# Moving batch 1's norm check and batch 0's first block scaling to VectorE, with new load times and pairs of score units, in a fused attention and FFN kernel

## The chip, the cores and the metric

The kernel runs on one core of one Trainium2 chip. The metric is device time in microseconds (us): the median of several executions. Engine names: PE is TensorE's matrix multiplication (PEld its weight loads, which overlap it), DVE is VectorE, ACT is ScalarE, POOL is GpSimd, SP is SyncE, which here only issues DMA transfers.

## The reference, cut to what matters

Eight batches of causal attention with a decay bias (8 heads, 576 positions, 64 columns per head) feed an RMS norm and a gated FFN over 4608 tokens.

```python
scores = scale * q @ k.T                                  # per batch and head
scores = where(causal, -1e9, scores + minimum(-(cum_i - cum_j), 0))
attn   = softmax(scores)                                  # [8, 8, 576, 576]
x      = (attn @ v) -> [4608, 512]
xn     = x / sqrt(mean(x*x) + 1e-6) * rms_g
out    = (silu(xn @ w_gate) * (xn @ w_val)) @ w_out       # d_ff = 1536
```

Of the kernel before, what the change touches and what calls it, by code (L numbers as in the profile page):

```python
# [270 lines left out]
def kernel(  # L271
# [13 lines left out]
    fp32 = mybir.dt.float32  # L285
    bf16 = mybir.dt.bfloat16
    i32 = mybir.dt.int32
    AF = mybir.ActivationFunctionType
    ALU = mybir.AluOpType
    AX = mybir.AxisListType  # L290

    B, H, S, D = q.shape
    DM = 512
    DF = 1536
# [3 lines left out]
    KC = 9  # L298
# [12 lines left out]
    NRUN = 2  # L311
    LEAD = 0.5
    MARGIN = 3.0
    NTWO = 2
    NPE = 3

    pers = ctx.enter_context(tc.tile_pool(name="pers", bufs=1))
# [17 lines left out]
    half = pers.tile([BH, 1], fp32, name="half")  # L335
    wT = pers.tile([128, NB, BH], bf16, name="wT")
    nrm = pers.tile([128, 2, B, 3], fp32, name="nrm")
    rnrm = pers.tile([128, NRUN, 5], fp32, name="rnrm")
    rtop = pers.tile([128, 1], fp32, name="rtop")
    top = pers.tile([128, 2], fp32, name="top")  # L340
    mhalf = pers.tile([128, 3], fp32, name="mhalf")
# [40 lines left out]
    def I(eng, method, us, key=None, kind=None, dma=0.0, lags=(1.2, 1.2), **kw):  # L382
        outs = [kw[n] for n in ("out", "accum_out") if n in kw]
        ins = [a for n, a in kw.items()
               if n not in ("out", "accum_out") and isinstance(a, (bass.AP, View))]
        f = getattr(ENG[eng], method)
        o = R.add(eng, us, lambda: f(**{n: real(a) for n, a in kw.items()}), outs, ins, key=key,  # L387
                  lat=LAT[eng], kind=kind, dma=dma,
                  name=outs[0].bank.name if isinstance(outs[0], View) else outs[0].name)
        o.lags = lags  # L390
        return o

    def fill(eng, ap, value, us, key=None):
        f = ENG[eng].memset
        return R.add(eng, us, lambda: f(ap, value), [ap], [], key=key, lat=LAT[eng], name=ap.name)
# [34 lines left out]
    def load_runs(b, which, h0, h1, key, part=0):  # L430
        c0, c1 = PARTS[part] if b == 0 else (0, KC)
        p0 = KP * which
        us = ((1.2, 1.25)[part] * (h1 - h0) / 4) if b == 0 else 3.05 * (h1 - h0) / 8
        return I("pool", "dma_start", 0.7, key=key, dma=us, lags=(1.1, 1.2),
                 out=raw[b][part][p0 : p0 + KP, h0:h1, :, :].rearrange("p h c d -> p h (c d)"),
                 in_=(k, q)[which][b, h0:h1, KP * c0 : KP * c1, :].rearrange(
                     "h (p c) d -> p h (c d)", c=c1 - c0))
# [9 lines left out]

    def load_w(which, lo, hi, key):
        if which == 2:
            return I("pool", "dma_start", 0.84, key=key, dma=7.2 * (hi - lo) / 12,  # L450
                     out=wout_sb[:, lo:hi, :],
                     in_=moe_w_out[lo * 128 : hi * 128, :].rearrange("(fc p) d -> p fc d", p=128))
        dst, src = ((wg_sb, moe_w_gate), (wv_sb, moe_w_val))[which]
        return I("pool", "dma_start", 0.76, key=key, dma=8.1 * (hi - lo) / DF,
                 out=dst[:, :, lo:hi],
                 in_=src[:, lo:hi].rearrange("(cc p) f -> p cc f", p=128))

# [17 lines left out]
    def prep_cast(b, key):  # L475
        for sc in range(NB):
            n = 128 if sc < 4 else 64
            for src, dst, out in ((k_nat, k_bf, KT[b % 2]), (q_nat, q_bf, QT[b % 2])):
                I("dve", "tensor_copy", 0.34, key=key + sc, out=dst[0:n, sc], in_=src[0:n, sc])
                I("sp", "dma_start_transpose", 1.31, key=key + sc, dma=0.65,  # L480
                  lags=(0.5, 0.9 + 0.6 * MARGIN),
                  out=out[:, :, sc * 128 : sc * 128 + n], in_=dst[0:n, sc])
# [5 lines left out]
        I("act", "activation", 1.17 if w > DM else 0.74, key=key, out=sq_scr[0:n, 0:w], in_=src,  # L488
          func=AF.Square, accum_out=nrm[0:n, which, b, i : i + 1])

    def raw_norm(b, key):
        src = flat[b]
        for i in range(5):
            w = min(1024, H * KC * D - 1024 * i)
            I("act", "activation", 1.17 if w > DM else 0.74, key=key, out=sq_scr[:, 0:w],
              in_=src[:, 1024 * i : 1024 * i + w], func=AF.Square,
              accum_out=rnrm[:, b, i : i + 1])

    def prep_v(b, sc, eng, key):
        n = 128 if sc < 4 else 64  # L500
# [15 lines left out]
    def decay(key):  # L516
        I("dve", "tensor_scalar", 0.5, key=key, out=s_all, in0=s_all, scalar1=0.0, scalar2=None,
          op0=ALU.max)
        I("dve", "tensor_tensor_scan", 1.3, key=key, out=cum, data0=ones[:, 0:1].to_broadcast([BH, S]), data1=s_all, initial=0.0,
          op0=ALU.mult, op1=ALU.add)  # L520
        I("dve", "tensor_scalar", 0.1, key=key, out=half, in0=cum[:, S - 1 : S], scalar1=-0.5,
          scalar2=None, op0=ALU.mult)
        I("act", "activation", 0.7, key=key, kind="exp", out=w_row[:, 0:S], in_=cum, func=AF.Exp,
          bias=half, scale=1.0)
        tp = lay(bank("w", 1), fp32, "p (c b) -> p c b", n=NB * BH, c=NB)
        mms(0.6, [(tp[:, sc, :], w_row[:, sc * 128 : (sc + 1) * 128], ident_f, sc == 0,
                   sc == NB - 1, True) for sc in range(NB)], key=key)
        I("dve", "tensor_copy", 0.42, key=key, out=wT, in_=tp)
        return tp
# [125 lines left out]
    def att_out(b, tb, key):  # L655
        x = x_blk[b % 2][:, tb, :]
        if b >= NPE:
            p0 = 64 if tb == 4 else 0
            I("dve", "scalar_tensor_tensor", 0.66, key=key, out=x, in0=x,
              scalar=al[b % 2][:, 1, tb : tb + 1], in1=gB, op0=ALU.mult, op1=ALU.mult)  # L660
            c0 = b * S + tb * 128
            I("sp", "dma_start_transpose", 1.31, key=key - 3, dma=0.65, lags=(0.5, 0.9 + 0.6 * MARGIN),
              out=xnT[:, :, c0 : c0 + 128 - p0], in_=x_blk[b % 2][p0:128, tb, :])
            return
        if b == 0 and tb in (1, 3):
            I("dve", "tensor_scalar", 0.3, key=key, out=x, in0=x,
              scalar1=al[b % 2][:, 1, tb : tb + 1], scalar2=None, op0=ALU.mult)
        else:
            I("act", "activation", 0.72, key=key, out=x, in_=x, func=AF.Copy,
              scale=al[b % 2][:, 1, tb : tb + 1])  # L670
        p0 = 64 if tb == 4 else 0
        X = lay(bank("xt", 2) if b == 0 else small_bank(), bf16, "p (c t) -> p c t", n=DM, c=CC)
        mms(0.22, [(X[:, cc, :], x_blk[b % 2][:, tb, cc * 128 : (cc + 1) * 128], ident_bf,
                    cc == 0, cc == CC - 1, True) for cc in range(CC)], key=key)
        c0 = b * S + tb * 128
        I("dve", "tensor_tensor", 0.6, key=key, out=xnT[:, :, c0 : c0 + 128 - p0],
          in0=X[:, :, p0:128], in1=g_sb.unsqueeze(2).to_broadcast([128, CC, 128 - p0]),
          op=ALU.mult)
# [101 lines left out]
        fill("dve", t[64:128, 4, :, :], 0.0, 0.5, key=-90)  # L780
    fill("dve", mhalf, -0.5, 0.06, key=-90)
    fill("dve", nrm, 0.0, 0.08, key=-90)
    wP = decay(-95)
    for hp in range(HP):
        prep_transpose(0, hp, -80 + hp)
# [7 lines left out]
    norms = attention(0, -78, 3, 4)  # L793
    for o in vops[2:]:
        R.after(o, norms[3])
    raw_norm(0, 20)
    kq1 = [load_runs(1, w, h, h + 4, -45) for h in (0, 4) for w in range(2)]
    v1 = load_rows(v_nat[1 % len(v_nat)], v, 1, "pool", -44)
    w2 = [load_w(2, 6 * i, 6 * i + 6, -40) for i in range(2)]
# [4 lines left out]
    for c in range(NCH):  # L804
        K = PER * c
        plan = first if c == 0 else halves if c < 4 else whole
        for i, (o, n, f0) in enumerate(plan):
            ffn1_group(c, o, n, f0, K + STEP * 96 * i / len(plan))
        b = c + 1
        if b < B:  # L810
            if b < NRUN:
                for hp in range(HP):
                    prep_transpose(b, hp, K + hp)
            else:
                prep_cast(b, K - 14)
            if b < NRUN:
                raw_norm(b, K + 18)
            else:
                for i in range(3):
                    for w in range(2):  # L820
                        prep_norm(b, w, i, K + 20 + 2 * i)
            prep_w(b, "pool", K - 10)
            vops = [prep_v(b, sc, "pool", K - 8 + sc) for sc in range(NB)]
        if b + 1 < B:
            n = b + 1
            K2 = K - 14 + LEAD
            for sc in range(NB):
                for dst, src in ((k_nat, k), (q_nat, q)):
                    o = load_row(dst, src, n, sc, "sp", K2 + sc)
                    if n == NRUN:  # L830
                        R.after(o, *vops)
            lv = [load_row(v_nat[n % len(v_nat)], v, n, sc, "sp", K2 + 6 + sc) for sc in range(NB)]
            if n == NRUN:
                R.after(gl, *lv)
        if c == B - 1:
            check_decay(K + 10)
            check_all(K + 20)
        ffn2(c, K + STEP * 96, STEP)
        if b < B:
            attention(b, K + 1, 2.6, 2 if b > 3 else 4)  # L840
# [175 lines left out]
```

## The kernel before: the parts that the change touches

All work is written as operations with an estimated duration and a key. A planner written in Python replays them by these estimates, and from that it fixes the order on each engine and the places where PE gets dummy matmuls (`spin`) so that its clock stays up. The estimates therefore change no instruction, but they change the order of thousands.

```python
def load_runs(b, which, h0, h1, key, part=0):        # k and q of batches 0 and 1
    ...
    us = ((1.2, 1.25)[part] * (h1 - h0) / 4) if b == 0 else 3.05 * (h1 - h0) / 8
    return I("pool", "dma_start", 0.7, key=key, dma=us, lags=(1.1, 1.2), ...)

def raw_norm(b, key):                                # sums of squares for a range check
    src = flat[b]
    for i in range(5):
        w = min(1024, H * KC * D - 1024 * i)
        I("act", "activation", 1.17 if w > DM else 0.74, key=key, out=sq_scr[:, 0:w],
          in_=src[:, 1024 * i : 1024 * i + w], func=AF.Square,
          accum_out=rnrm[:, b, i : i + 1])

def att_out(b, tb, key):                             # scale a finished block of x by 1/rms
    x = x_blk[b % 2][:, tb, :]
    ...
    if b == 0 and tb in (1, 3):
        I("dve", "tensor_scalar", 0.3, key=key, out=x, in0=x,
          scalar1=al[b % 2][:, 1, tb : tb + 1], scalar2=None, op0=ALU.mult)
    else:
        I("act", "activation", 0.72, key=key, out=x, in_=x, func=AF.Copy, scale=...)
    # then: 4 PE transposes into PSUM, and one DVE product into xnT, the FFN's input

two = 2 if b >= NTWO else 1                          # NTWO = 2: score units in pairs from batch 2

def spin(b):                                         # a dummy matmul
    nc.tensor.matmul(b[:, 0:256], lhsT=still[:, 0:128], rhs=still, start=True, stop=True)
```

On POOL are the causal masks (`affine_select` on the exponentials `Ea` to `Eh`) and, from batch 1 on, the products of v with the decay weights (`vwb`).

## Time and profile before

| | before |
|---|---|
| median of 4 executions (358.43 to 359.1) | 358.69 us |
| span in the profiled execution | 356.3 us |
| PE busy | 342.1 us, 96% of the span |
| DVE / ACT / POOL busy | 70% / 65% / 38% |
| first attention-times-v matmul | 14.72 us |
| first FFN matmul | 23.50 us |

Since PE is at 96%, the time is PE's work, plus its idle time, plus whatever its work costs more at a lower clock. The lines that carry this stand in the prediction (in a timeline: start, duration, engine, line, operation, what it writes and reads). One more view of before is needed later, the timeline at 20 us (start, duration, engine, line, operation, what it writes and reads). It has the one scaling of a batch 0 block that DVE did already:

```profile
20.54 0.84 POOL L387 DMA_DIRECT2D wv_sb<-in_moe_w_val_dram  x1
20.61 0.45 DVE L387 TENSOR_SCALAR x_blka<-x_blka,ala 128x512 bf16<-128x512 bf16 x1
```

The scaling and a DMA issue of POOL run side by side, and the scaling takes 0.45 us. The same operation at 31.1 us took 0.35 us. I saw no meaning in this difference when I predicted.

### The profile page before, as it was taken

To read this page: it belongs to the slowest core of one execution; us is meant where nothing else is said; L and a number is where in the kernel's file an instruction comes from. 1 tells how busy PE (TensorE), PEld (TensorE's weight loads), DVE (VectorE), ACT (ScalarE), POOL (GpSimd) and SP (SyncE) were. 2 spreads that over 40 slices of the span, in tenths; PEclk is the share of its full clock that TensorE was granted. 3 is DMA by queue.
4 is the path that set the end of the run, shared out by engine and by line. 5 is a ranking of instruction groups with operands and counts; after the bars stand their busy time and mean duration, and the time that the engine had idled before them with its cause. 6 is when DMAs were issued, how large, how long until landed. Compare 5 with 4: busy or idle time off the path is not lost.

```text
span 356.3 us, 8029 instructions
## 1 busy us (share of the span) xinstructions
PE 342.1 (96%) x3016; PEld 209.5 (59%) x3016; DVE 250.4 (70%) x495; ACT 229.8 (65%) x472; POOL 134.9 (38%) x217
## 2 busy tenths in 40 slices
PE   5988999999999999999999999999999999999995
PEld 4667775698569874887544454455445444444443
DVE  4678856698748995879687868887588657806840
ACT  2688899595777995857685668666898433224321
POOL 8996377321381349013910293029325100000000
PEclk9799999999999999999999999999999999999999
DMA  7999999999899997998999996889730250020002
GB/s 116 182 183 209 224 200 213 182 215 187 177 185 213 179 193 135 211 175 156 153 215 156 182 159 159 193 166 133 195 62 2 32 156 2 0 89 31 0 31 94
DMA packets 140613, 51.14 MB, mean 144 GB/s; under 512 B 127380, under 2 KB 135320, under 8 KB 140568
## 3 DMA queue, kind: packets, MB, share of 16 engines
q1 hardware_dynamic: 131832, 41.13, 60.7%
q0 software_dynamic: 8736, 9.44, 16.0%
q8 instruction: 25, 0.41, 0.5%
q14 instruction: 20, 0.16, 0.2%
HBM read 38.16 MB, written 9.44 MB: 134 GB/s over the span
## 4 chain that ended last, share of the span: by engine, by line
PE 84%; DVE 6%; POOL 3%; issue 3%; ACT 2%; DMA 1%; SPq 0%; POOLq 0%; ACTq 0%; DVEq 0%
PE psa L404 11%; PE psd L404 11%; PE pse L404 11%; PE psh L404 10%; PE psg L404 10%; PE psb L404 10%; PE psc L404 9%; PE psf L404 8%; DMA q_nat<-in_q_dram 1%; DVE x_blka L387 1%; DVE x_blkb L387 1%; POOL q_nat L387 1%; ACT Ee L387 1%; DVE Hs L387 1%; PE psd L843 1%
## 5 line engine op out<-in xcount | busy, mean ns | idle before, releaser
L404 PEld LDWEIGHTS <-wg_sb 128*128 128x128 bf16 x624 | 60.0, 98 | 33.8 <-issue 2.1
L404 PEld LDWEIGHTS <-wv_sb 128*128 128x128 bf16 x624 | 59.8, 98 | 32.3 <-issue 1.5
L404 PEld LDWEIGHTS <-Hs 128*128 128x128 bf16 x444 | 41.4, 98 | 42.5
L387 POOL TENSOR_SCALAR_AFFINE_SELECT Eb<-Eb 128x512 bf16<-128x512 bf16 x8 | 5.4, 679 | 80.7 <-ACT Eb L387 80.7
L387 POOL TENSOR_TENSOR vwb<-v_nata,wT 128x512 bf16<-128x512 f32 (+1 forms) x20 | 20.4, 1047 | 0.0
L387 ACT ACTIVATE sq_scr<-x_blkb 128x512 bf16<-128x512 bf16 x20 | 12.7, 633 | 11.7 <-DVE x_blkb L387 11.3
L387 DVE SCALAR_TENSOR_TENSOR x_blkb<-x_blkb,alb,gB 128x512 bf16<-128x512 bf16 x15 | 12.2, 862 | 10.7 <-POOL alb L387 10.7
L404 PE MATMUL psd<-wout_sb,Hs 128*128 128x512 bf16 (+1 forms) x84 | 18.5, 364 | 0.0
L404 PE MATMUL psa<-wout_sb,Hs 128*128 128x512 bf16 x72 | 17.8, 379 | 0.0
L404 PE MATMUL pse<-xnT,wg_sb 128*128 128x256 bf16 (+1 forms) x100 | 17.6, 311 | 0.2 <-DVE u_sba L387 0.2
L404 PE MATMUL psh<-xnT,wv_sb 128*128 128x256 bf16 (+1 forms) x100 | 17.5, 311 | 0.2 <-DVE x_blkb L387 0.2
L404 PE MATMUL psa<-xnT,wv_sb 128*128 128x256 bf16 (+1 forms) x104 | 17.6, 306 | 0.0
L387 ACT ACTIVATE sq_scr<-x_blka 128x512 bf16<-128x512 bf16 x18 | 11.3, 630 | 9.3 <-DVE x_blka L387 8.9
L404 PE MATMUL pse<-wout_sb,Hs 128*128 128x512 bf16 x72 | 17.2, 379 | 0.0
L404 PE MATMUL psf<-xnT,wg_sb 128*128 128x256 bf16 (+1 forms) x88 | 16.5, 321 | 0.6 <-DVE xnT L387 0.6
L404 PE MATMUL psb<-xnT,wv_sb 128*128 128x256 bf16 (+1 forms) x88 | 16.5, 321 | 0.0
L387 ACT ACTIVATE sq_scr<-q_bf 128x1024 bf16<-128x1024 bf16 (+1 forms) x18 | 16.4, 909 | 0.1
L387 ACT ACTIVATE sq_scr<-k_bf 128x1024 bf16<-128x1024 bf16 (+1 forms) x18 | 16.3, 908 | 0.0
L387 DVE CAST q_bf<-q_nat 128x512 bf16<-128x512 f32 (+1 forms) x30 | 16.0, 532 | 0.6 <-DMA q_nat<-in_q_dram 0.6
L387 POOL TENSOR_TENSOR vwa<-v_nata,wT 128x512 bf16<-128x512 f32 (+1 forms) x15 | 15.8, 1078 | 0.9 <-DMA v_nata<-in_v_dram 0.7
L404 PE MATMUL psd<-xnT,wv_sb 128*128 128x256 bf16 (+1 forms) x88 | 14.5, 302 | 0.0
L404 PE MATMUL psb<-xnT,wg_sb 128*128 128x256 bf16 (+1 forms) x88 | 14.5, 302 | 0.0
(471 smaller groups left out, 879.4 us busy)
## 6 DMA issues: line engine op xcount, KB each, us to landing
v_nata<-in_v_dram SPq DMA_DIRECT2D x24, 256.0 KB, 5.1
k_nat<-in_k_dram SPq DMA_DIRECT2D x24, 256.0 KB, 3.7
q_nat<-in_q_dram SPq DMA_DIRECT2D x24, 256.0 KB, 4.3
out_dram<-osba SPq DMA_DIRECT2D x12, 256.0 KB, 2.3
out_dram<-osbb SPq DMA_DIRECT2D x12, 256.0 KB, 2.5
out_dram<-osbc SPq DMA_DIRECT2D x11, 256.0 KB, 2.3
v_nata<-in_v_dram POOLq DMA_DIRECT2D x8, 256.0 KB, 10.4
wout_sb<-in_moe_w_out_dram POOLq DMA_DIRECT2D x2, 768.0 KB, 16.6
```

The source lines that it names most:

```text
L387: o = R.add(eng, us, lambda: f(**{n: real(a) for n, a in kw.items()}), outs, ins, key=key, lat=LAT[eng], kind=kind, dma=dma, name=outs[0]. ...
L404: nc.tensor.matmul(out, lhsT=lhsT, rhs=rhs, start=st, stop=sp)
L843: nc.tensor.matmul(b[:, 0:256], lhsT=still[:, 0:128], rhs=still, start=True, stop=True)
```

## The change

Its intent is to take work off ACT, which was at 96% in two windows of batch 1, and to start the FFN earlier. It has five parts:

- (a) batch 1's norm check goes from ACT (5 pieces) to DVE (9 pieces of 512 columns)
- (b) batch 1's score units go in pairs
- (c) batch 0's first block of x is scaled on DVE
- (d) the planner gets new load times
- (e) batch 2's casts get a later key

What the change's name calls "v of batch 1 between the out weights' halves" is already in the load list of the kernel before; the diff does not touch it.

```diff
-    NTWO = 2
+    NTWO = 1
-    rnrm = pers.tile([128, NRUN, 5], fp32, name="rnrm")
+    rnrm = pers.tile([128, NRUN, 9], fp32, name="rnrm")
...  load_runs
-        us = ((1.2, 1.25)[part] * (h1 - h0) / 4) if b == 0 else 3.05 * (h1 - h0) / 8
+        us = ((1.05, 1.25)[part] * (h1 - h0) / 4) if b == 0 else 2.85 * (h1 - h0) / 8
...  load_w: 7.2 -> 7.5 for the out weights; lags=(1.2, 1.6) for the gate and value weights
...  prep_cast
-   I("dve", "tensor_copy", 0.34, key=key + sc, ...)
+   I("dve", "tensor_copy", 0.34, key=key + sc + (12 if b == NRUN else 0), ...)
...  raw_norm, new branch
+            else:
+                I("dve", "scalar_tensor_tensor", 0.66, key=key, out=x, in0=x, scalar=1.0, in1=x,
+                  op0=ALU.mult, op1=ALU.mult, accum_out=rnrm[:, b, i : i + 1])
...  att_out
-        if b == 0 and tb in (1, 3):
+        if b == 0 and tb in (0, 1, 3):
...  in the loop over batches (batch 1)
-                raw_norm(b, K + 18)
+                raw_norm(b, K + 23, "dve")
```

More of the change, by code (lines that the diff above doesn't have):

```diff
@@ L449, in load_w @@
         if which == 2:
-            return I("pool", "dma_start", 0.84, key=key, dma=7.2 * (hi - lo) / 12,
+            return I("pool", "dma_start", 0.84, key=key, dma=7.5 * (hi - lo) / 12,
                      out=wout_sb[:, lo:hi, :],
@@ L453, in load_w @@
         dst, src = ((wg_sb, moe_w_gate), (wv_sb, moe_w_val))[which]
-        return I("pool", "dma_start", 0.76, key=key, dma=8.1 * (hi - lo) / DF,
+        return I("pool", "dma_start", 0.76, key=key, dma=8.1 * (hi - lo) / DF, lags=(1.2, 1.6),
                  out=dst[:, :, lo:hi],
@@ L478, in prep_cast @@
             for src, dst, out in ((k_nat, k_bf, KT[b % 2]), (q_nat, q_bf, QT[b % 2])):
-                I("dve", "tensor_copy", 0.34, key=key + sc, out=dst[0:n, sc], in_=src[0:n, sc])
+                I("dve", "tensor_copy", 0.34, key=key + sc + (12 if b == NRUN else 0), out=dst[0:n, sc], in_=src[0:n, sc])
                 I("sp", "dma_start_transpose", 1.31, key=key + sc, dma=0.65,
@@ L489, in prep_norm, with raw_norm @@
           func=AF.Square, accum_out=nrm[0:n, which, b, i : i + 1])
-    def raw_norm(b, key):
-        src = flat[b]
-        for i in range(5):
-            w = min(1024, H * KC * D - 1024 * i)
-            I("act", "activation", 1.17 if w > DM else 0.74, key=key, out=sq_scr[:, 0:w],
-              in_=src[:, 1024 * i : 1024 * i + w], func=AF.Square,
-              accum_out=rnrm[:, b, i : i + 1])
+    def raw_norm(b, key, eng):
+        w = 1024 if eng == "act" else DM
+        for i in range(-(-H * KC * D // w)):
+            x = flat[b][:, w * i : min(w * i + w, H * KC * D)]
+            if eng == "act":
+                I("act", "activation", 1.17 if x.shape[1] > DM else 0.74, key=key,
+                  out=sq_scr[:, 0 : x.shape[1]], in_=x, func=AF.Square,
+                  accum_out=rnrm[:, b, i : i + 1])
+            else:
+                I("dve", "scalar_tensor_tensor", 0.66, key=key, out=x, in0=x, scalar=1.0, in1=x,
+                  op0=ALU.mult, op1=ALU.mult, accum_out=rnrm[:, b, i : i + 1])
     def prep_v(b, sc, eng, key):
@@ L782 @@
     fill("dve", nrm, 0.0, 0.08, key=-90)
+    fill("dve", rnrm, 0.0, 0.06, key=-90)
     wP = decay(-95)
@@ L795 @@
         R.after(o, norms[3])
-    raw_norm(0, 20)
+    raw_norm(0, 20, "act")
     kq1 = [load_runs(1, w, h, h + 4, -45) for h in (0, 4) for w in range(2)]
```

## The prediction

> **What bounds the kernel now.** I read the engine totals first, then ten-microsecond windows, then the waits of PE alone, then the stretches in which PE is not full. The totals:
>
> ```profile
> PE 342.1 (96%) x3016; PEld 209.5 (59%) x3016; DVE 250.4 (70%) x495; ACT 229.8 (65%) x472; POOL 134.9 (38%) x217
> ```
>
> PE is the bound. The windows (columns: us, then busy time of PE, PEld, DVE, ACT and POOL with instruction counts, granted clock, DMA share, GB/s) show where it is not full:
>
> ```profile
> 10.00:20.00 10.00, 9.12 (x188) 5.76 (x189) 7.02 (x23) 7.10 (x21) 9.83 (x16) 0.79 1.19 175
> 20.00:30.00 10.00, 9.38 (x134) 7.83 (x131) 8.14 (x20) 7.08 (x16) 9.71 (x19) 1.00 1.16 196
> 30.00:40.00 10.00, 8.86 (x95) 7.58 (x95) 8.52 (x14) 9.62 (x20) 5.25 (x10) 1.00 1.19 208
> 40.00:50.00 10.00, 8.84 (x216) 6.79 (x218) 6.12 (x10) 8.66 (x17) 4.18 (x6) 1.00 1.18 213
> 50.00:60.00 10.00, 9.23 (x118) 6.48 (x117) 5.76 (x17) 9.69 (x21) 8.54 (x16) 1.00 1.07 210
> 60.00:70.00 10.00, 10.00 (x76) 6.03 (x75) 7.73 (x19) 6.05 (x14) 3.18 (x7) 1.00 1.23 203
> ```
>
> From 20 to 60 us PE is idle 0.62 + 1.14 + 1.16 + 0.77 = 3.7 us. From 60 to 350 the windows add up to 1.6 us of idle time. The tail after PE's last work, at 351.95 in the chain that ended last, is 4.3 us, and the change does not touch it. So there are two places to win: the 23.5 us before the first FFN matmul, where PE counts as busy only because it spins on dummy matmuls (line 843), and those 3.7 us. ACT is at 96% in two of these windows while DVE is below 62% in two. That imbalance is what the change aims at. What PE itself waited for:
>
> ```profile
> PE psa L402 <- POOL ident_F masks.py:199: 2.5, 1, 2.5
> PE psg L402 <- DVE x_blka L387: 1.1, 1, 1.1
> ...
> PE pse L402 <- issue: 0.7, 1, 0.7
> PE psf L404 <- DVE xnT L387: 0.6, 1, 0.6
> PE psa L404 <- DVE x_blkb L387: 0.5, 1, 0.5
> PE psd L404 <- ACT Ee L387: 0.5, 1, 0.5
> ```
>
> Only the last of these is an ACT wait; 1.1 us is batch 0's second half coming through DVE at 31.5 us, and 0.7 us has no releaser. The 2.5 us lie at 5.3 to 7.8 us, before any attention. In the chain that ended last (start, us, what) the start phase also holds
>
> ```profile
> 13.01 1.88 PE psd L843 x11
> ```
>
> eleven dummy matmuls that delay batch 0's first attention-times-v: its masks, its v and the scores are there at 13.0 us, yet it begins at 14.7.
>
> **What the Trainium skill says.** "TensorE: Matmul & The Clock Gate", section "Step-by-step: what each phase is for": matmuls stay in program order. So a dummy matmul that the kernel's planner has placed is paid in full, and an order chosen from wrong load times costs real waits; the 1.88 us above agree. The same page, "What's actually happening": the array runs at half its clock until it has been kept busy. Here a dummy of 256 columns took 1.88 / 11 = 0.171 us at a granted clock of 0.79 in that window, against 0.109 us (0.87 us for 8) in the FFN. "ScalarE: Activation LUTs", section "What ACT_TABLE_LOAD costs", gives 186 ns plus 0.833 ns per column for an instruction with immediate scale and bias, 1.04 us at 1024; the trace has 1.06 for the norm squares. "VectorE: DVE Perf Modes", "The perf-mode tier table", has tensor_scalar at four times the base rate in bf16; the trace has 0.35 us for it at 512 columns, against 0.72 to 0.76 us on ACT. The table does not list scalar_tensor_tensor; the trace has 0.69 us.
>
> **The change, part by part.**
>
> (a) Norm check of batch 1 from ACT to DVE. ACT's rows for it (the accumulator reads that follow each are left out):
>
> ```profile
> 38.84 1.06 ACT L387 ACTIVATE sq_scr<-k_nat 128x1024 bf16<-128x1024 bf16 x1
> ...
> 41.58 1.06 ACT L387 ACTIVATE sq_scr<-k_nat 128x1024 bf16<-128x1024 bf16 x1
> ...
> 52.97 1.06 ACT L387 ACTIVATE sq_scr<-k_nat 128x1024 bf16<-128x1024 bf16 x1
> ...
> 54.15 1.06 ACT L387 ACTIVATE sq_scr<-k_nat 128x1024 bf16<-128x1024 bf16 x1
> ...
> 55.33 0.63 ACT L387 ACTIVATE sq_scr<-k_nat 128x512 bf16<-128x512 bf16 x1
> ```
>
> With the reads, four take about 1.15 us and one 0.73: 5.3 us off ACT. DVE gets nine pieces of 512 columns. One such instruction (square of x_blka at 28.48) holds DVE 0.62 us from start to next start: 9 x 0.62 = 5.6 us. DVE's own gaps from 44 to 60 us (0.4 + 3.1 + 0.7 + 1.5 + 1.0 + 0.9) are 7.6 us, so this should fit. Of PE's waits it can take the 0.5 us at 48.9 (ACT's exps) and part of those at 52 to 56 (0.2 + 0.55 + 0.2). I count 0.7 us.
>
> (b) Scores of batch 1 in pairs. A lone unit, with the change-over from and to FFN matmuls, takes 0.42 us (FFN due to end at 49.80, next work at 50.22); a pair takes 0.65 (45.30 to 45.95). But the trace already shows three accidental pairs in batch 1 (45.4, 47.8, 51.6) and only two lone units: five groups become four, 2 x 0.42 - 0.65 = 0.2 us.
>
> (c) Batch 0's first x block scaled on DVE instead of ACT. Before, ACT does it from 20.68 to 21.44 and DVE fills the time with two v products until 22.17; then come two xnT evictions of 0.6 us each and the first FFN matmul at 23.50. On DVE the two scalings end near 21.3, and the evictions could start at about 21.4 to 21.8. Gain 0.4 to 0.8 us, counted as 0.4, because one v product may still slip in.
>
> (d) New load times in the planner (1.05 for 1.2 us per first load of batch 0, and others). No load is changed by that, only order and number of dummies. Following the planner's rule by hand for the kernel before: transposes of heads 0 to 3 are due at 6.77 us, the small matmul that needs ident_F at 6.49, so it goes first. That is the 2.5 us wait, as ident_F is only there at 7.76. With 1.05 the transposes are due at 6.47 and go first. Their data should be there at about 6.0 (issued at 2.17, 3.8 us to landing by the DMA table), so the four copies of the first two head pairs leave the path; but the transposes of w still follow ident_F, and the scores follow them, so I expect only 0.5 us here. And v is expected 0.6 us earlier, so three to four of the eleven dummies should go: 3.5 x 0.17 = 0.6 us. Together 1.1 us, but not all of it reaches the FFN, since weights, k, q and v of batch 1 come over DMA engines that are full (share over 1 from 10 to 60 us) and do not move. Counted: 0.8 us.
>
> (e) Casts of batch 2 twelve planning units later. They ran from 63.72 us, after the loads, in a stage in which PE is full; their first scores come after 85. Counted 0, with a risk of some tenths. The title's "v of batch 1 between the out weights' halves" is already in the load list of the kernel before, and the trace has it so (half of the out weights at 26.7, v, the other half at 39.7). 0.
>
> Sum: 0.7 + 0.2 + 0.4 + 0.8 = 2.1 us; 358.71 - 2.1 = 356.6 us.
>
> **The rivals.** (1) The start gains nothing that lasts: what PE wins before 24 us it waits for later, because loads of batch 1 and the out weights (landing 15.2 to 18.1 us after issue) arrive when they did. Then (a), (b) and a part of (c) remain, about 357.7 us. For it: full DMA engines, 208 to 213 GB/s from 30 to 60. Against it: PE has FFN work for 21 us from batch 0 alone, and half the out weights by about 43 us. (2) DVE becomes the bound of batch 1: its nine pieces come between attention's divisions and the FFN's products, and the reload of k_nat for batch 2 must now wait for DVE, which delays its casts and transposes. DVE in 30 to 40 is at 85%. If PE waits 1 to 2 us more, the time is 357.5 to 359. (3) It goes better: all eleven dummies and the whole wait at 31.5 go. Even with all PE idle time from 20 to 350 us gone (5.3 us) and 1.5 us more of the start, it would be near 352: faster by more than 2% needs below 351.5.
>
> **Range and chances.** 356.6 is the sum. The low end, 354.8, adds the full start gain and half of the remaining idle time; the high end, 358.4, is rival (1) or (2) with little left. The order from 100 us on will be shuffled, which may move it by some tenths either way. Under 351.5 or over 366 I see no mechanism: 1% each.
>
> **What would show it.** In the changed trace: the wait of PE for ident_F at 5 to 8 us gone or behind the first transposes; fewer than eleven dummies before the first attention-times-v, which starts near 13.6 instead of 14.7; the first FFN matmul near 22.3 instead of 23.5; ACT below 9 us in the windows 40 to 60 and DVE above 7; no wait for exps Ee; PE idle from 20 to 60 us near 3 us. If the FFN starts earlier but PE's idle time from 20 to 60 us grows as much, rival (1) was right. If PE waits for DVE, or the casts of batch 2 come after 68 us and PE waits for scores of batch 2 near 90, rival (2). The prediction is wrong if the start phase does not move, or if a new order leaves PE waiting after 60 us by a microsecond or more.

## The result, and the profile after

The changed kernel takes 368.76 us (367.94 to 369.48, 4 executions) against 358.69. The ratio is 1.0279, with a 95% interval of 1.0253 to 1.0305. Ratios here are the mean time of one kernel's fast executions over that of the other's in the same rounds, so they are not quite the ratio of the medians quoted beside them. Executions over 1.5% slower than the fastest of the same kernel are left out of the means. The span of the profiled execution grew from 356.3 to 367.7 us.

The windows of the changed kernel (columns as in the prediction) say where:

```profile
20.00:30.00 10.00, 6.46 (x72) 4.87 (x69) 7.29 (x9) 3.41 (x7) 7.50 (x15) 0.67 1.16 190
30.00:40.00 10.00, 8.29 (x89) 7.15 (x87) 8.02 (x17) 7.22 (x15) 6.33 (x13) 0.99 1.19 207
50.00:60.00 10.00, 7.33 (x79) 5.50 (x79) 6.44 (x12) 4.93 (x10) 5.13 (x5) 0.83 0.48 91
60.00:70.00 10.00, 9.27 (x103) 5.80 (x101) 9.46 (x26) 5.24 (x12) 6.27 (x8) 1.00 0.75 159
```

PE lost 2.9 us of busy time in the window from 20 us, and in that same window its clock fell to 0.67 of full speed, where it had 1.00 before. It lost another 1.9 us in the window from 50, again with a low clock (0.83), and 0.7 in the one from 60. Even ACT, which was to be relieved, is now half empty. What PE waited for (line, tile written, releaser: us in total, times, longest):

```profile
PE psg L402 <- issue: 3.4, 1, 3.4
PE psg L402 <- DVE x_blka L387: 2.8, 1, 2.8
PE psb L404 <- DVE u_sbc L387: 1.3, 1, 1.3
PE psa L404 <- DVE x_blkb L387: 1.3, 1, 1.3
...
PE pse L402 <- POOL ident_F masks.py:199: 1.1, 1, 1.1
```

Two single waits of about three microseconds each are new. The last line is good news: the wait for `ident_F` fell from 2.5 to 1.1 us, as predicted. The first attention-times-v began at 13.32 us (predicted: near 13.6). But the first FFN matmul came at 26.28 us, not near 22.3.

A trace is one execution, and the start differs between executions of one and the same kernel. Runs 11 and 17 below are the same kernel: attention-times-v began at 13.67 us in one trace and at 14.96 in the other, where the granted clock from 11 to 14 us was 0.82 and 0.50. It was 0.50 in the trace of before and 0.65 in this one, so a part of the 1.4 us gained is luck with the clock. At 0.50 on both sides, the kernels with the old load times (before, runs 7, 13, 16, 17) began it at 14.72 to 15.45 us, and those with the new ones (runs 1, 3, 5, 9) at 13.50 to 14.38. That is a gain of about 1 us, as predicted.

**The wait for x_blka.** The timeline of the changed kernel around it:

```profile
19.98 0.83 POOL L387 DMA_DIRECT2D wv_sb<-in_moe_w_val_dram  x1
20.05 4.05 DVE L387 TENSOR_SCALAR x_blka<-x_blka,ala 128x512 bf16<-128x512 bf16 x2 [0.63 <-POOL ala L387]
20.83 0.90 POOL L387 TENSOR_SCALAR_AFFINE_SELECT Ee<-Ee 128x512 bf16<-128x512 bf16 x2
...
23.33 0.92 POOL L387 TENSOR_SCALAR_AFFINE_SELECT Eh<-Eh 128x512 bf16<-128x512 bf16 x2
24.02 0.68 DVE L387 TENSOR_TENSOR vwa<-v_nata,psf 128x512 bf16<-128x512 f32 x1
24.16 0.61 PE L402 MATMUL psg<-ident_bf,x_blka 128*128 128x128 bf16 x4 [2.80 <-DVE x_blka L387]
```

Two scalings of 0.35 us each, one after the other, hold DVE for 4.05 us. Taken apart they lasted 0.85 and 3.28 us. The first ends 0.1 us after POOL's DMA issue (20.81), the second at about 24.1, when a row of eight masks on POOL is nearly through. My reading is that DVE does not run slowly here but stands still; run 4 tests it. Meanwhile PE has nothing to do, its clock falls, and the next FFN matmuls take almost twice as long:

```profile
26.28 1.91 PE L404 MATMUL psb<-xnT,wg_sb 128*128 128x256 bf16 x8
...
30.43 1.04 PE L404 MATMUL pse<-xnT,wv_sb 128*128 128x256 bf16 x8
```

The same eight matmuls take 1.91 us at 26.28 and 1.04 us at 30.43.

**The wait that has no releaser ("issue").** It falls in the middle of a run of equal little transposes whose inputs are all there:

```profile
49.06 0.19 PE L402 MATMUL psc<-ident_bf,k_nat 64*64 64x64 bf16 x1
52.66 0.19 PE L402 MATMUL psg<-ident_bf,k_nat 64*64 64x64 bf16 x1 [3.42 <-issue]
```

After it the clock is low again: eight FFN matmuls take 1.74 us at 53.89 and 1.91 us at 55.43.

**The norm pieces.** The list of instructions on `k_nat` (duration in ns: shortest, median, longest), then two of them with POOL's row beside them:

```profile
L387 DVE SCALAR_TENSOR_TENSOR k_nat<-k_nat x9: 681/762/1514, 53.9 to 68.7; 128x512 bf16<-128x512 bf16 x9
...
56.65 4.92 POOL L387 TENSOR_TENSOR vwb<-v_nata,wT 128x512 bf16<-128x512 f32 x4
58.12 1.11 DVE L387 SCALAR_TENSOR_TENSOR k_nat<-k_nat 128x512 bf16<-128x512 bf16 x1
59.16 1.51 DVE L387 SCALAR_TENSOR_TENSOR k_nat<-k_nat 128x512 bf16<-128x512 bf16 x1
```

A piece takes 0.68 us where it is alone, and 1.11 and 1.51 us beside POOL's products.

### The profile page after: what moved, and what is told of

Its sections match the earlier page's. It is cut to its first block, busy times and chain, and to the rows that moved or that the text cites. A ratio compares the mean times of both kernels' runs of the same rounds, so it can differ in the third digit from the quotient of the medians.

```text
span 367.7 us, 8052 instructions
## 1 busy us (share of the span) xinstructions
PE 346.8 (94%) x3013; PEld 211.6 (58%) x3013; DVE 261.9 (71%) x515; ACT 224.7 (61%) x461; POOL 134.4 (37%) x217
## 4 chain that ended last, share of the span: by engine, by line
PE 78%; DVE 10%; POOL 4%; issue 3%; ACT 2%; DMA 2%; DVEq 0%; POOLq 0%; ACTq 0%
PE psg L404 12%; PE pse L404 10%; PE psa L404 10%; PE psc L404 10%; PE psb L404 9%; PE psd L404 9%; PE psh L404 8%; PE psf L404 8%; DMA q_nat<-in_q_dram 2%; DVE x_blka L387 2%; DVE Hs L387 2%; DVE u_sbc L387 1%; DVE x_blkb L387 1%; ACT sq_scr L387 1%; POOL q_nat L387 1%
## 5 line engine op out<-in xcount | busy, mean ns | idle before, releaser
L404 PE MATMUL psf<-xnT,wv_sb 128*128 128x512 bf16 (+1 forms) x108 | 21.6, 332 | 0.0
L404 PE MATMUL psh<-xnT,wv_sb 128*128 128x256 bf16 (+1 forms) x108 | 19.4, 319 | 0.3 <-DVE u_sbc L387 0.3
L404 PE MATMUL psb<-xnT,wg_sb 128*128 128x256 bf16 (+1 forms) x80 | 16.3, 340 | 2.4 <-DVE u_sbc L387 1.3
L404 PE MATMUL psc<-xnT,wg_sb 128*128 128x512 bf16 (+1 forms) x92 | 18.5, 333 | 0.0
L404 PE MATMUL psg<-wout_sb,Hs 128*128 128x512 bf16 x72 | 17.5, 379 | 0.0
L404 PE MATMUL psa<-xnT,wg_sb 128*128 128x256 bf16 (+1 forms) x92 | 16.5, 315 | 0.0
L404 PE MATMUL pse<-xnT,wg_sb 128*128 128x256 bf16 (+1 forms) x88 | 16.5, 321 | 0.0
L404 PE MATMUL psd<-xnT,wv_sb 128*128 128x256 bf16 (+1 forms) x88 | 16.5, 321 | 0.0
L404 PE MATMUL psg<-xnT,wv_sb 128*128 128x512 bf16 (+1 forms) x80 | 16.5, 337 | 0.0
L404 PE MATMUL psg<-xnT,wg_sb 128*128 128x256 bf16 (+1 forms) x100 | 15.5, 294 | 0.2 <-DVE u_sba L387 0.2
```

The lines of the kernel that those rows point to most:

```text
L404: nc.tensor.matmul(out, lhsT=lhsT, rhs=rhs, start=st, stop=sp)
```

## The experiments

The theory that came out of these views has three parts:

1. DVE and POOL exclude each other at a port to SBUF, and the change puts DVE instructions that need this port next to rows of POOL work.
2. PE's stop without a releaser is a late instruction fetch.
3. The norm pieces suffer from (1), and stand in front of attention's divisions.

The rivals: the new order itself is bad (loads, pairs, casts); or DVE simply has too much work.

For part 1 the Trainium skill has a page that I had not read before I predicted: "SBUF — State Buffer", section "Who interferes with whom". It says that DVE in its two-port perf mode (copies, casts, `tensor_scalar` unless it also writes out its accumulator), and DVE with two SBUF inputs against a POOL instruction that reads SBUF, need a pair of ports that POOL also uses; whoever issues first has it for the whole instruction, and the other is fully blocked. Runs 1 to 7 test consequences of that.

For part 2, the page "Runtime: NRT & Kernel Launch", section "Instruction fetch mechanics", says that each engine's instructions are fetched in blocks of 16 KiB (256 instructions) over a DMA queue of the sequencer's own, and calls this mostly hidden. The trace agrees on the blocks: one queue of kind "instruction" moved 25 packets of 16384 bytes.

**Run 1: the changed kernel with the first block's scaling back on ACT.**

```diff
-        if b == 0 and tb in (0, 1, 3):
+        if b == 0 and tb in (1, 3):
```

> The changed kernel with one part undone: batch 0's first x block is scaled on ACT again, as before. Theory (the second scaling on DVE waits 3.3 us because POOL holds the shared SBUF port through eight mask instructions in a row, and all that follows, a cold clock and a long instruction-fetch stall, comes of the 3 us shift): first FFN matmul near 22.8 instead of 26.3 us, no DVE scaling above 1 us at 20 us, time 357 to 361 us. Rival (the norm check on DVE beside POOL delays batch 1 and is the main loss): time stays at 364 us or more.

Measured: 359.23 us median (358.86, 358.91, 359.55 and one of 363.8), ratio 1.0035 [0.9961, 1.011]. The first FFN matmul came at 23.20 us, and the stop in batch 1 was 1.3 us instead of 3.6. One line is worth 1.0279 - 1.0035 = 2.4%, 8.8 us of 358.7. This is by far the largest part of the loss. The outlier keeps the interval wide.

**Run 2: the same part alone in the kernel before.**

```diff
-        if b == 0 and tb in (1, 3):
+        if b == 0 and tb in (0, 1, 3):
```

> The kernel before with that one part alone: batch 0's first x block scaled on DVE. Theory: if its second DVE scaling falls beside POOL's run of masks as in the changed kernel, it takes 3 us or more and the time rises by 4 to 8 us; rival: at most 1 us of change. If POOL's order differs so that the masks do not run there, the scaling takes under 1 us and the time stays near 358.5.

Measured: 363.27 us; one execution of 359.65, four between 363.2 and 363.89. Ratio 1.0117 [1.009, 1.0143]. Two outcomes of one program fit a race for a lock. The trace is of the fast execution:

```profile
20.63 0.84 POOL L387 DMA_DIRECT2D wv_sb<-in_moe_w_val_dram  x1
20.69 1.33 DVE L387 TENSOR_SCALAR x_blka<-x_blka,ala 128x512 bf16<-128x512 bf16 x2 [1.12 <-POOL ala L387]
...
21.48 0.32 POOL L387 TENSOR_SCALAR_AFFINE_SELECT Ee<-Ee 128x128 bf16<-128x128 bf16 x1
21.73 1.02 POOL L387 TENSOR_SCALAR_AFFINE_SELECT Ef<-Ef 128x512 bf16<-128x512 bf16 x2
```

The two scalings took 1.33 us together. The second ended at 22.02, inside POOL's second mask, and this mask took 0.78 us, where the same one took 0.64 in the changed kernel: here DVE got in between two masks, and POOL seems to have waited. No trace of a slow execution exists, so that DVE lost the race in those is argued, not shown.

**Run 3: the changed kernel with the norm check back on ACT.**

```diff
-                raw_norm(b, K + 23, "dve")
+                raw_norm(b, K + 18, "act")
```

> The changed kernel with the norm check of batch 1 back on ACT, nothing else undone. Theory (scaling is the main cause): scaling still takes over 3 us, first FFN matmul still near 26.3, time 365 to 369. Rival (norm check is the main loss): time falls to 362 or less.

Measured: 366.14 us, ratio 1.0179 [1.0138, 1.0219]. The norm check on DVE costs the changed kernel 1.0% (3.6 us by the ratios, 2.6 by the medians). The scalings still took 4.07 us. Not all of the 1.0% need be the norm pieces' own: in this trace the stop in batch 1 is 2.2 us instead of 3.6, and the clock from 50 to 60 us is 1.00 instead of 0.83.

**Run 4: the changed kernel with the same instructions in the same order, but the two scalings in a form without the two-port mode.** They also write out an accumulator that nobody reads.

```diff
+            if tb in (0, 1):
+                I("dve", "tensor_scalar", 0.3, key=key, out=x, in0=x,
+                  scalar1=al[...], scalar2=0.0, op0=ALU.mult, op1=ALU.add,
+                  accum_out=spare[:, tb : tb + 1])
```

> The changed kernel in exactly its order, only the two DVE scalings of batch 0's first half in a form that also writes out an accumulator, which by the skill's SBUF page does not run in a two-port mode. Theory (the shared port): each takes about 0.7 us whatever POOL does, first FFN matmul near 23.5 instead of 26.3, time lower by 3 to 8 us. Rival (DVE waits for something else at 20 to 24 us, such as a semaphore from POOL or the alpha values): the scaling or the wait before it still takes 3 us, and the time stays at 368.

Measured: 361.09 us (360.88 to 361.24), ratio 1.0051 [1.0026, 1.0076]. This is the deciding run, since the order of every engine is that of the changed kernel (compared instruction by instruction), and only the form of two instructions differs; each has the read-out of its accumulator (0.09 us) behind it. Its list of instructions on the tile, and its windows:

```profile
L388 DVE TENSOR_SCALAR_CACHE_REDUCE x_blka<-x_blka,ala x2: 744/746/747, 19.9 to 20.6; 128x512 bf16<-128x512 bf16 x2
...
20.00:30.00 10.00, 8.68 (x121) 7.22 (x117) 8.82 (x22) 5.72 (x14) 8.98 (x17) 1.00 1.12 191
```

This form takes 0.75 us beside POOL's work; the other takes 0.35 us where it does not wait. Beside the same POOL work the pair now takes 1.4 us instead of 4.05, because it does not wait. The first FFN matmul came at 23.17 us instead of 26.28, the clock stayed at 1.00, and the stop in batch 1 shrank to 0.8 us. Together that is 2.3%, 8.2 us.

**Run 5: run 4 and the norm check back on ACT.** (The edits of runs 3 and 4 together.)

> The changed kernel with the two DVE scalings in the form without the shared port, and the norm check of batch 1 back on ACT: what is left of the change are the new load times, the pairs, and the casts. Theory (the 2 us by which the no-port run is still slower than before come of nine norm pieces on DVE, which stretch beside POOL and stand in front of attention's divisions): 357.5 to 359.5 us, and the 1.1 us wait of PE near 61 us gone. Rival (the casts or the new order lose it): 360.5 us or more.

Measured: 358.19 us, ratio 0.9982 [0.9962, 1.0003]. With both contentions gone, loads, pairs and casts included, the kernel is back at the time of before. Its trace shows no stop in batch 1. From run 4, another session, to this one the norm check's place is worth 1.0051 - 0.9982 = 0.7%, 2.5 us.

**Run 6: run 4 with the nine norm pieces on DVE, but with one input instead of two.** They then sum instead of summing squares. This blunts the range check on purpose; the output stays correct.

```diff
-                I("dve", "scalar_tensor_tensor", 0.66, key=key, out=x, in0=x, scalar=1.0, in1=x,
-                  op0=ALU.mult, op1=ALU.mult, accum_out=rnrm[:, b, i : i + 1])
+                I("dve", "tensor_scalar", 0.66, key=key, out=x, in0=x, scalar1=1.0, scalar2=0.0,
+                  op0=ALU.mult, op1=ALU.add, accum_out=rnrm[:, b, i : i + 1])
```

> The no-port run again in exactly its order, the nine norm pieces as instructions with one input (sums in place of squares, so the check is blunted on purpose; the output is unchanged). Theory (two SBUF inputs contend with POOL): all nine take 0.7 to 0.75 us, none above 1, and the time falls by 0.5 to 2 us below 361.1. Rival (what costs is their place in DVE's queue, not their stretching): pieces shorter, time within 0.5 us of 361.1.

Measured: 359.46 us, ratio 1.0026 [1.0008, 1.0044]. The pieces, in the list of instructions on their tile:

```profile
L388 DVE TENSOR_SCALAR_CACHE_REDUCE k_nat<-k_nat x9: 676/680/681, 45.9 to 58.6; 128x512 bf16<-128x512 bf16 x9
```

All nine take 0.68 us, whatever POOL does. PE's wait for batch 1's divisions near 60 us is 0.4 us in this trace and 1.1 in run 4's. Against run 4 the time is lower by 1.6 us by the medians and 0.9 by the ratios (two sessions), but the intervals of the ratios overlap: that the unstretched pieces win time is likely and not shown. Runs 5 and 6 are of one session, and their intervals do not overlap. Between them lie 1.0026 - 0.9982 = 0.4%, 1.6 us, with no piece stretched. (A stop of 0.8 us in batch 1, which run 5's trace lacks, may be half of it.) So the port makes at most a part of what the norm check costs in this order, and the second rival (DVE has too much work) keeps a share.

**Run 7: the kernel before with the norm check on DVE and nothing else.** (The `raw_norm` part of the diff.)

> The kernel before with the norm check of batch 1 on DVE alone. The prediction's step (a) said 0.7 us faster. Theory: pieces beside POOL's v products take 1 us or more, and the time rises by 0.5 to 3 us. Rival (the step was right): 357.5 to 358.5.

Measured: 362.63 us, ratio 1.0107 [1.0085, 1.0129]: alone it costs 4 us. Its instructions on the tile, then the longest piece with POOL's masks beside it:

```profile
L387 DVE SCALAR_TENSOR_TENSOR k_nat<-k_nat x9: 681/1108/3740, 47.3 to 66.2; 128x512 bf16<-128x512 bf16 x9
...
55.07 3.74 DVE L387 SCALAR_TENSOR_TENSOR k_nat<-k_nat 128x512 bf16<-128x512 bf16 x1
55.38 0.63 POOL L387 TENSOR_SCALAR_AFFINE_SELECT Ee<-Ee 128x512 bf16<-128x512 bf16 x1
...
57.63 1.32 POOL L387 TENSOR_SCALAR_AFFINE_SELECT Eh<-Eh 128x512 bf16<-128x512 bf16 x2
```

A piece of 0.68 us took 3.74 and ended at 58.81, near the end of a row of seven masks. It is the picture of the scalings again, with another instruction; no run undoes the stretching alone in this kernel, so the cause of its 4 us is argued from the trace. PE waited 1.5 and 1.1 us for divisions (`x_blkb`) of batch 1, where before had one wait of 0.5 us. "DVE has room for 5.6 us" was true by the busy times and of no use.

**Runs 8 and 14: the changed kernel with 28 one-column matmuls (56 instructions with their weight loads) ahead of the first dummy matmul**, which moves every later instruction of PE by 56 places against the fetch blocks.

```diff
+        if first_spin.pop() if first_spin else False:
+            for i in range(28):
+                nc.tensor.matmul(b[0:32, 0:1], lhsT=still[:, 0:32], rhs=still[:, 0:1],
+                                 start=True, stop=True)
```

> The changed kernel with 28 one-column dummy matmuls, 56 instructions, more at PE's start. In the kernel before, the changed one and four variants PE stops at its instruction 1217 in the trace, in the middle of the transposes of batch 1, until 2.4 to 2.7 us after a 16 KB instruction transfer of 256 instructions began. Theory (PE waits for its instructions): the stop is again at instruction 1217, now 56 instructions earlier in the transposes. Rival (the stop belongs to the transposes, such as a missing load): it stays at the same transpose, which is now instruction 1273.

> The changed kernel with 28 one-column matmuls ahead of its first dummy matmul, as in run 8, now in rounds. Theory (the stop of 3.6 us at instruction 1217 and the cold clock behind it are a part of the loss that the wait for the shared port doesn't explain): median 364 to 366, that is 3 to 5 us under the changed kernel, and no stop over 1 us at a 256-instruction step in batch 1. Rival (run 8 was a lucky single execution): 367 to 369.

Measured: 364.8 us in one execution (run 8), then 364.99 (364.41 to 366.36), ratio 1.016 [1.0133, 1.0187] in rounds (run 14). The scalings still blocked DVE (first FFN matmul at 26.27 us in run 14), the stop in batch 1 was gone (run 8) or down to 0.3 us (run 14), and with it 1.0279 - 1.016 = 1.2%, 4.3 us. A part of that is the clock after the stop, which from 50 to 60 us was 1.00 in run 14 and 0.83 in the changed kernel. What I had expected of the stop's place in run 8 did not come true: it did not move to another place, it disappeared. That fits a block edge which now comes earlier in PE's work, where the fetch has time.

Counting PE's trace records from 0 (matmuls, weight loads and the few others of its queue), the stop sits before record 1217 in all kernels without the 56 instructions, whatever was changed, except run 5, which has none; and 1217 = 193 + 4 x 256. The 193 is read from this one place: at the other steps of 256, before and the changed kernel show no gap of over 0.31 us. The raw trace gives for that block (us; "crossed" is PE's start of record 961, one block earlier; "fetch" is the start of the next 16 KiB packet of the instruction queue after it):

```
run                        crossed   fetch after   PE stops at 1217 for
before                       39.99        1.70            0.85
changed kernel               44.56        5.43            3.61
4  (no two-port mode)        39.40        2.91            0.82
7  (norm alone)              40.40        2.06            1.15
10 (load times alone)        39.34        3.37            2.52
11 (pairs alone)             40.09        1.81            1.24
14 (changed, shifted)        43.48        1.66            0.31
12 (before, shifted)         38.53        0.89            0.00
15 (load times, shifted)     38.12        0.66            0.00
```

In the traces of all 15 kernels without the 56 instructions (13 runs, before and the changed one) PE began record 1217 2.3 to 2.9 us after the packet began, with stops from 0 to 3.6 us; in runs 8, 12 and 15 it came there later than that, 3.2 to 4.3 us after, and did not stop. So a stop becomes long in two ways: PE runs through the block quickly (little transposes), or the packet begins late. In the changed kernel it began 5.43 us after the crossing, while half of the out weights (issued at 40.30) filled the DMA engines. That these transfers are what delays the packet is argued from the times, not shown by a run.

**Run 9: the changed kernel with the edits of runs 1 and 3**, which leaves loads, pairs and casts.

> The changed kernel with both DVE parts undone (first x block and norm check of batch 1 on ACT): left are the new load times, the pairs and the casts. The prediction gave these 0.8 + 0.2 + 0 us: 357.7. Theory: the losses all came of the two DVE parts, so 357.5 to 358.7. Rival: one of the rest also costs, 359.5 or more.

Measured: 358.62 us, ratio 1.0004 [0.9987, 1.0021]. The other three parts together are worth nothing.

**Runs 10 and 15: the load times alone in the kernel before, and the same with the 56 instructions of run 8.**

```diff
-        us = ((1.2, 1.25)[part] * (h1 - h0) / 4) if b == 0 else 3.05 * (h1 - h0) / 8
+        us = ((1.05, 1.25)[part] * (h1 - h0) / 4) if b == 0 else 2.85 * (h1 - h0) / 8
...  load_w as in the change
```

> The kernel before with the new load times in its planner alone. Prediction's step (d): first attention-times-v near 13.6 instead of 14.7 us and 0.8 us faster, 357.8. Rival (1) of the prediction: the start gains 0.5 to 1 us, but the time stays within 0.3 us of before.

> The kernel before with the new load times alone (run 10: 361.75) and the same 28 matmuls. Theory (what the load times cost is mainly a longer stop at instruction 1217, 2.5 us instead of 0.85): 359.0 to 360.3, so 1.5 to 2.7 us under run 10. Rival (the loss lies in the new order of the work): 361 to 363.

Measured: 361.75 us, ratio 1.0107 [1.0077, 1.0136], and 362.2 us, ratio 1.0092 [1.0055, 1.0128]. In run 10's trace attention-times-v began at 13.69 us, a full microsecond earlier, and the first FFN matmul only 0.3 us earlier (23.19 for 23.50); but these are single traces with different clocks at the start. At the like clock of 0.50 from 11 to 14 us, and with the first block scaled on ACT, the first FFN matmul came at 23.50 to 24.30 us with the old load times (before, runs 7, 13, 16, 17) and at 22.90 and 23.20 with the new ones (runs 9, 1), so some 0.7 us of the gain reaches it. The whole is slower all the same. In its waits the stop stands first:

```profile
PE psc L402 <- issue: 2.3, 1, 2.3
```

I held this stop for the cause. Run 15 takes it away, and the time stays: that theory fell. What is left in run 15's trace from 50 to 75 us is a wait of 0.9 us for the divisions (`x_blkb`), where before had 0.5, and after that many waits of 0.2 to 1 us. Which of them make up the 3.5 us is open.

**Runs 11 and 17: the pairs alone in the kernel before.**

```diff
-    NTWO = 2
+    NTWO = 1
```

> The kernel before with batch 1's scores in pairs alone. Prediction's step (b): 0.2 us faster. Rival: pairs wait for both units' k and q and need all four banks at once, so ACT's exps come later and the time rises by 0.5 us or more.

> Run 11 again, unchanged: the kernel before with the pairs alone. Theory (the pairs are worth 1 to 2 us, and moving the casts in run 16 took that away): ratio 0.993 to 0.997 again. Rival (run 11 was a good session, and pairs are worth nothing): ratio 0.998 to 1.002.

Measured: 357.09 us, ratio 0.9954 [0.9938, 0.9969], and in another session 356.29 us, ratio 0.9945 [0.993, 0.996]. This beats both kernels, by 1.6 and 2.0 us. Its window (run 17):

```profile
50.00:60.00 10.00, 10.00 (x91) 5.88 (x88) 5.66 (x16) 7.58 (x19) 4.99 (x8) 1.00 1.06 206
```

PE is full where it had 9.23 us. ACT fell from 9.69 to 7.58 us and POOL from 8.54 to 4.99, so that work moved to where it fits. The relief of ACT that the norm check was to bring came from the order.

**Run 12: the kernel before with the 56 instructions.** (The edit of run 8.)

> The kernel before with 28 one-column dummy matmuls (56 instructions) at PE's start, where PE waits 2.5 us for ident_F anyway. Theory (the 0.85 us stop at instruction 1217 is a wait for instructions, and where the block boundary falls decides its length): the stop is gone or under 0.3 us, and the time falls by up to 0.6 us, if the dummies fit in the wait. Rival: the stop stays at the same transpose.

Measured: 358.88 us, ratio 1.0011 [0.9987, 1.0034]. The stop of 0.85 us is gone, but there is no net gain, and the trace does not say why: attention-times-v began at 15.34 instead of 14.72 us, but run 13, without the 56 instructions, has 15.45 at the same clock.

**Runs 13 and 16: the casts alone, and casts with pairs.**

```diff
-                I("dve", "tensor_copy", 0.34, key=key + sc, ...)
+                I("dve", "tensor_copy", 0.34, key=key + sc + (12 if b == NRUN else 0), ...)
```

> The kernel before with nothing but the casts of batch 2 placed 12 later. Theory (the prediction's step on the casts, worth 0): within 0.4 us of the kernel before. Rival (the casts fall beside GpSimd's work later and are stretched to over 1 us, as one was in the changed kernel): over 1 us slower, with a cast of over 0.8 us in the trace.

> The kernel before with two parts of the change, the pairs (run 11: 357.09) and the casts of batch 2 placed later. Theory (casts worth 0): 356.7 to 357.6. Rival (the casts cost in this order): over 358.

Measured: casts alone 359.52 us, ratio 1.0012 [0.9992, 1.0033]. Casts and pairs 359.97 us, ratio 1.0025 [1.0, 1.005], where the pairs alone had 0.9954 and 0.9945. The prediction's 0 for the casts holds alone and fails beside the pairs, where they take back the whole gain of 1.6 to 2.0 us and more. The trace shows no cast over 0.86 us, and run 13's longest is as long (0.85); in the window from 80 to 90 us PE has 9.25 us in run 16 and 10.00 in run 11, so the loss shows there first. Which instruction starts it is open.

## Why the prediction was wrong, point by point

The prediction said 356.6 us, range 354.8 to 358.4, with 1% for slower by over 2%. The result is 368.76.

- **Step (c), the scaling on DVE, failed, with the wrong sign.** It counted two scalings "near 21.3" and 0.4 us of gain. They ended at about 24.1. Runs 1 and 4 put what the scaling costs at 8.8 and 8.2 us, and run 4 shows that the form of the two scalings alone makes this loss, as the SBUF page quoted above has it. The price of one instruction was taken from a row where POOL ran only tiny instructions beside it (0.35 us at 31.1 us; POOL's are 128x1 and 128x32). Of the 8 us, the wait itself explains 3.1 (first FFN matmul at 26.28 against 23.17 in run 4). The rest follows in time: a low clock for some 4 us of FFN work, in which matmuls take almost twice as long, and a stop in batch 1 of 3.6 us instead of 0.8, because, as I read it, everything now met another moment of the transfers. Of these only the stop was tested apart (run 14).
- **Step (a), the norm check, failed with the wrong sign.** "9 x 0.62 = 5.6 us fits in 7.6 us of gaps" gave -0.7 us. Measured: +4 us alone (run 7) and, within the change, 2.6 to 3.6 us (run 3) or 2.5 us (run 4 against run 5). Pieces took up to 1.5 us (in run 7 up to 3.7), and they stood ahead of the divisions that PE waits for. Of this, 1.6 us stay when no piece is stretched (run 6 against run 5), so the 5.6 us did not fit into DVE's gaps for nothing even without the stretching.
- **Step (d), the load times, was right about the start and wrong about its worth.** The `ident_F` wait fell (2.5 to 1.1 us) and attention-times-v began at 13.3 (predicted 13.6; luck in part, see above), with seven dummies before it instead of eleven. At a like clock some 0.7 us reached the FFN, near the 0.8 counted. But the order that came with it cost 3.3 to 3.8 us (runs 15 and 10), and that the prediction had at some tenths. The first rival, a gain lost later, was the right direction and too small.
- **Step (b), the pairs, was right in sign and too small:** 0.2 us predicted, 1.6 and 2.0 measured (runs 11 and 17). It counted change-overs on PE, and not what the order does to ACT and POOL in the next ten microseconds. That this is where the gain lies is read from run 17's window, not tested.
- **Step (e), the casts at 0,** held alone (run 13), and not beside the pairs (run 16).
- **The second rival (DVE becomes the bound of batch 1, up to 359)** was right in part. It named the engine that PE then waited for, DVE is at 9.46 us in the changed kernel's window from 60, and 1.6 us are left in run 6 with no piece stretched. What it did not see is the lock, which makes the 8 us of the scaling.
- **"Over 366 I see no mechanism"** was the worst sentence. The mechanism was in a page I had not opened, and in the trace as 0.45 us against 0.35.
- **One reading was loose:** the 0.79 beside the dummies of 0.171 us is the mean clock from 10 to 20 us. From 11 to 14 us, where most of them lie, it was 0.50.

The costs of single parts do not add up to 10 us, and cannot: undoing (c) wins 8 to 9 us, removing the stop 4.3, undoing (a) about 3. That is 16, because the stop became long through the delay of (c). The parts left over in run 9 are worth 0 together, though loads alone cost 3.5 and pairs alone win nearly 2.

## What to carry to other kernels

Before moving work to VectorE, look at what GpSimd does in the same stretch: a fast `tensor_scalar` or a two-input instruction there can wait for a whole row of GpSimd instructions, and a slower form without that mode can win by far. Where PE stops in a row of equal instructions without a releaser, move its instructions by some dozens of places and see whether the stop stays at its work, before looking for a semaphore. An order made from estimates can move the time by 1% with no instruction changed (run 10: 1.0107), so try each part alone: here one of five was worth keeping. And compare the starts of two traces only at a like granted clock.

## What the Trainium skill lacked or had wrong

- "SBUF — State Buffer", section "Who interferes with whom", agrees with the traces on who contends, but speaks of one instruction of waiting. Here DVE, once behind, waited for a row of POOL instructions: 3.28 us beside eight masks in the changed kernel, 3.74 us beside seven in run 7; in run 2 it got in after the first mask. The page should say that the loser may not get in between two instructions of the other engine.
- The same page, on DMA issued by POOL: it describes DVE starving the issue. Here the reverse shows: a scaling of 0.35 us took 0.85 us and ended 0.1 us after POOL's DMA issue of 0.83 us. Not every issue does this: in the kernel before it took 0.45 us and ended 0.3 us before the issue did. What decides is open.
- "Runtime: NRT & Kernel Launch", section "Instruction fetch mechanics", calls the fetch hidden. Here PE stopped 0.85 us in the kernel before and 3.6 us in the changed one before record 1217, taken for a block edge, as the packet began 1.7 and 5.4 us after PE had entered the block ahead of it; removing that stop in the changed kernel won 4.3 us. The page has no word on how late a fetch may come when the DMA engines are full.
- "VectorE: DVE Perf Modes", section "The perf-mode tier table", has no row for `tensor_scalar` with an accumulator (0.75 us for 128x512 bf16 here, against 0.35 without) nor for `scalar_tensor_tensor` (0.68 to 0.69 us).
